# A Fourier layer and two feed-forward blocks: table loads placed behind tiles, weight conversion placed later, planner wait 130 to 210

## The chip, the cores and the metric

The kernel runs on one core of one Trainium2 chip, as one launch. The metric is the device time of that launch in microseconds, lower being better. TensorE is called PE, VectorE DVE, ScalarE ACT, GpSimd POOL and SyncE SP, as in the profile.

## What is computed

Three layers in a row, on `x` of 4 x 3072 x 256 in float32:

```python
X = np.fft.rfft(x, axis=1)
Yr = Xr @ w_r - Xi @ w_i + b_r;  Yi = Xr @ w_i + Xi @ w_r + b_i
Y = soft_threshold(Yr, 0.01) + 1j * soft_threshold(Yi, 0.01)
y = np.fft.irfft(Y, n=3072, axis=1)
h = y @ w_in;  x2 = (h - tanh(h)) @ w_out
xk, xr = token_shift_mix(x2, mu_k), token_shift_mix(x2, mu_r)
out = sigmoid(xr @ w_r2) * (relu(xk @ w_k) ** 2 @ w_v)
```

## The kernel before

The work falls into three parts. The transform runs over four batches (`b`). Both Fourier transforms are products with tables: a transform of 3072 is split into 96 x 32. For each batch:

- `reg_a` (L435), stage A: eight loads of `x` (`load_x`, L391, issued by SP), for each two products with the table `f_sb`, each evacuated by ACT into one half of a tile `at` (L464), which is written to HBM (`adr`, L468; in batch 0 issued by ACT, in the later ones by SP). PE writes to two banks `a` in turn. Batch 0 takes plain float32 products, later batches a split into two parts (`xa`, `xb`).
- `reg_q` (L470): twelve loads of `adr` in another layout, the tiles `q` (L475, SP). Each reads what all eight `adr` writes of its batch have written, so the first one waits for the last write.
- `reg_unit` (L479), twelve units. PE multiplies `q` by the table `t` into a bank `g`; ACT and DVE split it into `xh` and `xl` (two buffers each); PE multiplies these by the weights `wh`, `wl` into a bank `y`; DVE adds `bias` (L529, L532) and applies the threshold; ACT and DVE split that into `zh` and `zl`; PE multiplies by the table `b` into a bank `v`; ACT evacuates it, and SP writes it to `vdr` (L555).
- `reg_ap` (L557): loads of `vdr` in a third layout, products with `e_sb`, writes of `ydr`.

Then follow the two feed-forward blocks (`reg_pair`, `reg_m2`), each over 24 chunks of 512 tokens, with products of 128x128 by 128x256 and 128x512. Meanwhile `reg_conv` (L597) takes the float weights apart, sixteen of them during the transform (raw loads by POOL, L613, DVE work, and writes by SP).

The tables come in seven groups (`groups`): `t2`, `t0`, `t4`, `t6`, `t10`, `t14`, `t18` for the first product of a unit and `b2`, `b0`, ... for its last; the number is the first pair of rows in the group, and units 3 and 4 (counted from 0) use `t6`, 5 and 6 `t10`, 7 and 8 `t14`, 9 to 11 `t18`. All of them, the two weights of the transform (a tile `v` each, split into `wh` and `wl` at L424 and L425), the four bias loads and `e_sb` are loaded by POOL.

The order of the instructions on each engine is made by a planner (`_Plan`, L149). Each operation has an engine, a cost, a priority number and the operations it depends on; the planner places them in a simulated time, in which a result is taken to be usable by another engine `SEM` = 130 ns after its end (L146). Only the order on each engine comes from the plan. What an instruction waits for on the chip is set by the tiles that it reads and writes. The entries that the kernel adds to `deps` by hand for the loads, at the end of the function (`early`, `load_t`, `load_b`), are known to the planner alone:

```python
for n, o in enumerate(early):
    o.deps.add(xt[0, 1 + n][0].readers[0])
for n, (g0, _) in enumerate(groups):
    p = UNITS.index(g0 // 2)
    for o, c in ((load_t[n], 4), (load_b[n], 6)):
        o.deps.add(first_mm[0, p - 2] if p > 1 else xt[0, c][0].readers[0])
```

Of the kernel before, what the change touches and what calls it, by code (L numbers as in the profile page):

```python
# [8 lines left out]
F32 = mybir.dt.float32  # L9
F32R = mybir.dt.float32r  # L10
I32 = mybir.dt.int32
ACTF = mybir.ActivationFunctionType
# [7 lines left out]
NP = 24  # L20
# [125 lines left out]
SEM = 130  # L146
# [165 lines left out]
def fourier_moe_kernel(tc, x, w_r, w_i, b_r, b_i, w_in, w_out, mu_k, mu_r, w_k, w_v, w_rr, c_f, c_e, c_t, c_b, out, nb=B, ydump=None):  # L312
# [22 lines left out]
    def tile_(pool_, shape, dtype, tag, bufs=1, ordered=True):  # L335
        return _Tile(pool_, shape, dtype, tag, bufs, ordered)
# [65 lines left out]
    wst, early = [], []  # L402
    for q, w in enumerate((w_r, w_i)):
        t = tile_(pl, [128, 2, D], F32, "v", 4)
        wst.append(t)
        dma("pool", lambda t=t, w=w: pool.dma_start(out=t(), in_=w.rearrange("(h p) e -> p h e", p=128)), -90, [t], [], 262144)
        early.append(plan.ops[-1])
    for o, r0, r1, src in ((bias, 0, 64, b_r), (bias, 64, 128, b_i), (bias0, 0, 65, b_r), (bias0, 65, 128, b_i)):
        dma("pool", lambda o=o, r0=r0, r1=r1, src=src: pool.dma_start(out=o()[r0:r1], in_=src.partition_broadcast(r1 - r0)), -59.5, [o], [], 65536)
    dma("pool", lambda: pool.dma_start(out=e_sb(), in_=c_e), -59.4, [e_sb], [], 36864)  # L410
    load_t, load_b = [], []

    def reg_tables(n):
        g0, g1 = groups[n]
        dma("pool", lambda: pool.dma_start(out=t_sb[n](), in_=c_t[:, g0:g1]), g0 / 2 - 60 + n, [t_sb[n]], [], 65536 * (g1 - g0))
        load_t.append(plan.ops[-1])
        dma("pool", lambda: pool.dma_start(out=b_sb[n](), in_=c_b[:, g0:g1]), -60 + n * 0.1, [b_sb[n]], [], 131072 * (g1 - g0))
        load_b.append(plan.ops[-1])

    for n in range(len(groups)):  # L420
        reg_tables(n)
    for q in range(2):
        cols = slice(q * D, q * D + D)
        op("act", c_act(512, False), lambda q=q, cols=cols: act.activation(out=wh()[:, :, cols], in_=wst[q](), func=ACTF.Copy), -50, [wh], [wst[q]])  # L424
        op("dve", c_dve(512), lambda q=q, cols=cols: dve.tensor_tensor(out=wl()[:, :, cols], in0=wst[q](), in1=wh()[:, :, cols].bitcast(F32), op=ALU.subtract), -50, [wl], [wst[q], wh])  # L425
# [9 lines left out]
    def reg_a(b):  # L435
        for c in range(8):
            a = tile_(px, [NP * 4, 4, D], F32, "at", AB)
# [39 lines left out]
    first_mm = {}  # L477

    def reg_unit(b, pos):  # L479
# [18 lines left out]
        first_mm[b, pos] = plan.ops[-1]  # L498
# [6 lines left out]
        op("act", c_act(128 * n, False), lambda: act.activation(out=xl()[:, 0:2 * n, 0:64], in_=xl()[:, 0:2 * n, 128:192].bitcast(F32), func=ACTF.Copy, scale=-1.0), z0 - K["x"], [xl], [])  # L505
        if u == 0:
            for o, src in ((xh0, xhc), (xl0, xlc)):
                for c0, k0, sc in ((1, 65, -1.0), (65, 1, 1.0)):
                    op("act", c_act(126, False), lambda o=o, src=src, c0=c0, k0=k0, sc=sc: act.activation(out=o()[:, :, c0:c0 + 63], in_=src[1]()[:, 0:2, k0:k0 + 63].bitcast(F32), func=ACTF.Copy, scale=sc), z0 - K["x"], [o], [src[0]])
# [85 lines left out]
    RAW0, RAW1 = 14, 6  # L595
# [51 lines left out]
    reg_q(0)  # L647
    for b in range(nb):
        for i in range(NU):
            reg_unit(b, i)  # L650
        if b == 0:
            for n, o in enumerate(early):
                o.deps.add(xt[0, 1 + n][0].readers[0])
            for n, (g0, _) in enumerate(groups):
                p = UNITS.index(g0 // 2)
                for o, c in ((load_t[n], 4), (load_b[n], 6)):
                    o.deps.add(first_mm[0, p - 2] if p > 1 else xt[0, c][0].readers[0])
# [394 lines left out]
```

## Time and profile before

| | us |
|---|---|
| median of three runs | 2008.94 (2005.75 to 2009.99) |
| the profiled execution, its own time | 2006.93 |
| its span, first to last instruction | 2005.1 |
| PE busy in the span | 1961.8 (98%) |
| DVE busy | 1599.4 (80%) |
| ACT busy | 1476.9 (74%) |
| POOL busy | 22.9 (1%) |

The profile is one execution. A busy PE is one that has a matmul in flight; the rest of the span, 43.3 us, is time in which PE had nothing to run. The granted clock is the share of TensorE's full 2.4 GHz that it was given, where 0.5 is 1.2 GHz. A wait is put down to what ended last. "us to landing" counts from the issue of a transfer to its completion.

### The profile page before, as it was taken

The page shows a single profiled execution, that of the slowest core. Times are in us where ns is not written, and L with a number is a line of the kernel's source. Part 1 is how long each engine was busy: PE and PEld are TensorE (multiplying, and loading weights), DVE is VectorE, ACT ScalarE, POOL GpSimd, SP SyncE. Part 2 cuts the span into 40 slices and gives each one's busy share as a digit, 9 for nine tenths or more (in the row PEclk, how much of TensorE's full clock was granted, in tenths as well). Part 3 has the DMA queues.
Part 4 walks back from the last instruction along what each step waited for, and adds up shares of the span by engine and source line. Part 5 has one row for each costly group of instructions (what it writes and reads, how often), then busy time and mean ns, then how long its engine had stood idle before and what let it go on. Part 6 is the DMA issues. An engine that isn't in the chain of part 4 may idle for free.

```text
span 2005.1 us, 36620 instructions
## 1 busy us (share of the span) xinstructions
PE 1961.8 (98%) x13760; PEld 1822.3 (91%) x13760; DVE 1599.4 (80%) x3107; ACT 1476.9 (74%) x3166; POOL 22.9 (1%) x42
## 2 busy tenths in 40 slices
PE   5999999999999999999999999999999999999998
PEld 3899989888888888888888888888999999999998
DVE  1688897788887878887878897779988888888885
ACT  3657566777777777777777787778877777777774
POOL 2000000000000000000000000000000000000000
PEclk8999999999999999999999999999999999999999
DMA  9699786511010101010101120001211111111101
GB/s 311 197 288 295 242 264 217 179 48 55 29 47 24 37 22 48 32 38 22 38 22 48 38 69 22 22 11 35 60 44 50 48 47 47 47 47 47 47 22 33
DMA packets 96194, 162.37 MB, mean 81 GB/s; under 512 B 11510, under 2 KB 56675, under 8 KB 96016
## 3 DMA queue, kind: packets, MB, share of 16 engines
q1 hardware_dynamic: 91008, 142.95, 22.8%
q0 software_dynamic: 4112, 13.93, 2.4%
q10 hardware_dynamic: 896, 3.15, 0.4%
q8 instruction: 108, 1.77, 0.4%
q14 instruction: 70, 0.57, 0.1%
HBM read 90.52 MB, written 69.47 MB: 80 GB/s over the span
## 4 chain that ended last, share of the span: by engine, by line
PE 89%; DVE 5%; DMA 3%; ACT 2%; issue 1%; SPq 0%; ACTq 0%; DVEq 0%
PE v L319 39%; PE y L319 20%; PE g L319 17%; PE a L319 14%; DVE hs L840 1%; DVE hs L799 1%; DVE yl L348 1%; DMA x<-in_x_dram 1%; DMA adr<-at 1%; DVE gl L348 1%; DMA ydr<-yt 0%; DMA out_dram<-ob 0%; DVE zl L348 0%; DMA vp<-vdr 0%; DMA yr<-ydr 0%
## 5 line engine op out<-in xcount | busy, mean ns | idle before, releaser
L345 ACT ACTIVATE gh<-hs 128x512 fp32r<-128x512 f32 x504 | 317.2, 629 | 139.2 <-PE v L319 131.4
L348 DVE TENSOR_TENSOR gl<-hs,gh 128x512 fp32r<-128x512 f32 x504 | 345.1, 685 | 79.5 <-ACT gh L345 79.1
L796 ACT ACTIVATE p<-g 128x256 f32<-128x256 f32 x864 | 318.7, 383 | 92.8 <-PE g L319 75.0
L840 DVE TENSOR_TENSOR hs<-hs,th 128x512 f32<-128x512 f32 x384 | 264.4, 689 | 122.1 <-ACT th L839 115.1
L319 PE MATMUL v<-gh,wl 128*128 128x512 f32 x768 | 303.6, 395 | 0.0
L319 PE MATMUL v<-gh,wh 128*128 128x512 f32 x768 | 303.3, 395 | 0.0
L319 PE MATMUL v<-gl,wh 128*128 128x512 f32 x768 | 300.0, 391 | 0.0
L839 ACT ACTIVATE th<-hs 128x512 f32<-128x512 f32 x384 | 241.5, 630 | 76.2 <-DVE hs L799 71.6
L799 DVE TENSOR_TENSOR hs<-y,p 128x256 f32<-128x256 f32 x588 | 241.4, 420 | 37.1 <-PE y L319 25.8
L319 PE MATMUL v<-ah,gh 128*128 128x256 f32 x768 | 217.5, 283 | 0.5 <-DVE ob L1004 0.5
L319 PE MATMUL v<-al,gh 128*128 128x256 f32 x768 | 217.3, 283 | 0.0
L319 PE MATMUL v<-ah,gl 128*128 128x256 f32 x768 | 217.3, 283 | 0.0
L319 PE MATMUL g<-yh,ah 128*128 128x256 f32 x648 | 183.2, 283 | 0.1
L319 PE MATMUL g<-yh,al 128*128 128x256 f32 x648 | 182.8, 282 | 0.0
L319 PE MATMUL g<-yl,ah 128*128 128x256 f32 x648 | 182.5, 282 | 0.0
L319 PEld LDWEIGHTS v<-gl,wh 128*128 128x128 f32 x768 | 144.4, 188 | 33.4
L319 PEld LDWEIGHTS v<-gh,wh 128*128 128x128 f32 x768 | 145.2, 189 | 18.1
L319 PEld LDWEIGHTS v<-gh,wl 128*128 128x128 f32 x768 | 145.2, 189 | 16.0
L319 PE MATMUL y<-yh,ah 128*128 128x256 f32 x496 | 149.8, 302 | 2.6 <-ACT hs L824 1.0
L319 PEld LDWEIGHTS v<-ah,gh 128*128 128x128 f32 x768 | 147.4, 192 | 0.8 <-DVE ob L1004 0.7
L319 PEld LDWEIGHTS v<-al,gh 128*128 128x128 f32 x768 | 147.4, 192 | 0.0
L319 PEld LDWEIGHTS v<-ah,gl 128*128 128x128 f32 x768 | 147.4, 192 | 0.0
(179 smaller groups left out, 4875.9 us busy)
## 6 DMA issues: line engine op xcount, KB each, us to landing
x<-in_x_dram SPq DMA_DIRECT2D x32, 384.0 KB, 5.2
q<-adr SPq DMA_DIRECT2D x48, 256.0 KB, 5.8
vdr<-v SPq DMA_DIRECT2D x48, 256.0 KB, 3.6
vp<-vdr SPq DMA_DIRECT2D x32, 384.0 KB, 6.3
ydr<-yt SPq DMA_DIRECT2D x64, 192.0 KB, 4.5
yr<-ydr SPq DMA_DIRECT2D x24, 512.0 KB, 4.0
xdr<-x SPq DMA_DIRECT2D x24, 512.0 KB, 3.1
xs<-xdr SPq DMA_DIRECT2D x20, 608.0 KB, 4.3
```

The costliest lines, as they stand in the source:

```text
L319: pe.matmul(out=o, lhsT=l, rhs=r, start=st, stop=en, **kw)
L345: op("act", c_act(n, psum), lambda: act.activation(out=o[1](), in_=i[1](), func=ACTF.Copy), prio, [o[0]], [i[0]])
L348: op("dve", c_dve(n), lambda: dve.tensor_tensor(out=o[1](), in0=i[1](), in1=h[1]().bitcast(F32), op=ALU.subtract), prio, [o[0]], [i[0], h[0]])
L796: op("act", c_act(HK, True), lambda: act.activation(out=o(), in_=p()[:, 0:HK], func=ACTF.Copy), prio, [o], [p])
L799: op("dve", c_dve(HK), lambda: dve.tensor_tensor(out=t()[:, half * HK:half * HK + HK], in0=p()[:, 0:HK], in1=s(), op=ALU.add), prio, [t], ...
L839: op("act", c_act(CK, False), lambda th=th, hs=hs: act.activation(out=th(), in_=hs(), func=ACTF.Tanh), z0, [th], [hs])
L840: op("dve", c_dve(CK), lambda th=th, hs=hs: dve.tensor_tensor(out=hs(), in0=hs(), in1=th(), op=ALU.subtract), z0, [hs], [th])
```

## The change

Five things are altered.

1. A helper `pool_after` puts a copy of one element of a given tile into a tile `gate` on POOL (L407 of the changed kernel). The loads that follow it in POOL's order start after that copy. The table, weight, bias and `e_sb` loads are spread behind nine such copies: three read tiles `at` of batch 0, one the first `q`, five the `xh` of units 0, 1, 3, 5 and 7.
2. The entries in `deps` that did this in the plan alone are gone.
3. The two weights are converted with priority -2 in place of -50.
4. `SEM` is 210 in place of 130, for every operation of the kernel.
5. `RAW0`, which says at which unit the plan lets the raw weight loads begin, is 12 in place of 14.

```diff
--- before.py
+++ after.py
@@ -143,7 +143,7 @@
     __slots__ = ("eng", "dur", "lat", "emit", "deps", "prio", "creates", "users", "nleft", "start", "end", "idx", "ready", "frees", "nbytes")
 
 
-SEM = 130
+SEM = 210
 
 
 class _Plan:
@@ -399,30 +399,32 @@
 
     for c in range(8):
         load_x(0, c)
-    wst, early = [], []
-    for q, w in enumerate((w_r, w_i)):
-        t = tile_(pl, [128, 2, D], F32, "v", 4)
-        wst.append(t)
-        dma("pool", lambda t=t, w=w: pool.dma_start(out=t(), in_=w.rearrange("(h p) e -> p h e", p=128)), -90, [t], [], 262144)
-        early.append(plan.ops[-1])
-    for o, r0, r1, src in ((bias, 0, 64, b_r), (bias, 64, 128, b_i), (bias0, 0, 65, b_r), (bias0, 65, 128, b_i)):
-        dma("pool", lambda o=o, r0=r0, r1=r1, src=src: pool.dma_start(out=o()[r0:r1], in_=src.partition_broadcast(r1 - r0)), -59.5, [o], [], 65536)
-    dma("pool", lambda: pool.dma_start(out=e_sb(), in_=c_e), -59.4, [e_sb], [], 36864)
-    load_t, load_b = [], []
-
-    def reg_tables(n):
+    wst = [tile_(pl, [128, 2, D], F32, "v", 4) for _ in range(2)]
+
+    def pool_after(t, view):
+
+        g = tile_(pl, [1, 1], F32, "gate", 2)
+        op("pool", 100, lambda: pool.tensor_copy(out=g(), in_=view(t())), -60, [g], [t])
+        return plan.ops[-1]
+
+    def pool_load(o, emit, nbytes, gate):
+        dma("pool", emit, -60, [o], [], nbytes, after=[gate] if gate else [])
+
+    def load_w(q, gate):
+        w = (w_r, w_i)[q]
+        pool_load(wst[q], lambda: pool.dma_start(out=wst[q](), in_=w.rearrange("(h p) e -> p h e", p=128)), 262144, gate)
+
+    def load_bias(gate):
+        for o, r0, r1, src in ((bias, 0, 64, b_r), (bias, 64, 128, b_i), (bias0, 0, 65, b_r), (bias0, 65, 128, b_i)):
+            pool_load(o, lambda o=o, r0=r0, r1=r1, src=src: pool.dma_start(out=o()[r0:r1], in_=src.partition_broadcast(r1 - r0)), 65536, gate)
+
+    def load_t(n, gate):
         g0, g1 = groups[n]
-        dma("pool", lambda: pool.dma_start(out=t_sb[n](), in_=c_t[:, g0:g1]), g0 / 2 - 60 + n, [t_sb[n]], [], 65536 * (g1 - g0))
-        load_t.append(plan.ops[-1])
-        dma("pool", lambda: pool.dma_start(out=b_sb[n](), in_=c_b[:, g0:g1]), -60 + n * 0.1, [b_sb[n]], [], 131072 * (g1 - g0))
-        load_b.append(plan.ops[-1])
-
-    for n in range(len(groups)):
-        reg_tables(n)
-    for q in range(2):
-        cols = slice(q * D, q * D + D)
-        op("act", c_act(512, False), lambda q=q, cols=cols: act.activation(out=wh()[:, :, cols], in_=wst[q](), func=ACTF.Copy), -50, [wh], [wst[q]])
-        op("dve", c_dve(512), lambda q=q, cols=cols: dve.tensor_tensor(out=wl()[:, :, cols], in0=wst[q](), in1=wh()[:, :, cols].bitcast(F32), op=ALU.subtract), -50, [wl], [wst[q], wh])
+        pool_load(t_sb[n], lambda: pool.dma_start(out=t_sb[n](), in_=c_t[:, g0:g1]), 65536 * (g1 - g0), gate)
+
+    def load_b(n, gate):
+        g0, g1 = groups[n]
+        pool_load(b_sb[n], lambda: pool.dma_start(out=b_sb[n](), in_=c_b[:, g0:g1]), 131072 * (g1 - g0), gate)
 
     fh = tile_(pt, [N1, 128], F32R, "fh")
     fl = tile_(pt, [N1, 128], F32R, "fl")
@@ -434,7 +436,7 @@
 
     def reg_a(b):
         for c in range(8):
-            a = tile_(px, [NP * 4, 4, D], F32, "at", AB)
+            a = at[b, c] = tile_(px, [NP * 4, 4, D], F32, "at", AB)
             for h in range(2):
                 p = bank("a")
                 t, tx = xt[b, c]
@@ -473,8 +475,6 @@
             t = tile_(pt, [128, 2, D], F32, "q", NU)
             qt[b, i] = t
             dma("sp", lambda t=t, u=u: sp.dma_start(out=t(), in_=rows[u]), base(b) + i - K["q"], [t], [adr[b]], 262144)
-
-    first_mm = {}
 
     def reg_unit(b, pos):
         n = 2
@@ -495,7 +495,6 @@
                     mm(px_()[:, o:o + 128], qs()[:, k, dh * 128:dh * 128 + 128], t_sb[g]()[:, ti, :], True, True)
 
         op("pe", 448 * n, e, z0 - K["b"], [px_], [qs] + [t_sb[g] for g, _ in ts_])
-        first_mm[b, pos] = plan.ops[-1]
         x3 = cut(px_, lambda r: r.rearrange("p (k c) -> p k c", k=4)[:, 0:2 * n])
         xhc = cut(xh, lambda r: r[:, 0:2 * n, 64:192])
         xlc = cut(xl, lambda r: r[:, 0:2 * n, 64:192])
@@ -503,6 +502,14 @@
         lo(xlc, x3, xhc, 256 * n, z0 - K["x"])
         op("act", c_act(128 * n, True), lambda: act.activation(out=xh()[:, 0:2 * n, 0:64], in_=x3[1]()[:, :, 64:128], func=ACTF.Copy, scale=-1.0), z0 - K["x"], [xh], [px_], seq=False)
         op("act", c_act(128 * n, False), lambda: act.activation(out=xl()[:, 0:2 * n, 0:64], in_=xl()[:, 0:2 * n, 128:192].bitcast(F32), func=ACTF.Copy, scale=-1.0), z0 - K["x"], [xl], [])
+        if b == 0 and pos in (0, 1, 3, 5, 7):
+            gate = pool_after(xh, lambda r: r[0:1, 0, 64:65].bitcast(F32))
+            n_ = (0, 1, 3, 5, 7).index(pos) + 2
+            if n_ > 2:
+                load_t(n_, gate)
+            load_b(n_, gate)
+            if pos == 3:
+                pool_load(e_sb, lambda: pool.dma_start(out=e_sb(), in_=c_e), 36864, gate)
         if u == 0:
             for o, src in ((xh0, xhc), (xl0, xlc)):
                 for c0, k0, sc in ((1, 65, -1.0), (65, 1, 1.0)):
@@ -592,7 +599,7 @@
     wdr = [_Tile(dram, None, None, None, 1, fixed=wdr_t[i]) for i in range(NW)]
 
     EARLY = 16
-    RAW0, RAW1 = 14, 6
+    RAW0, RAW1 = 12, 6
 
     def reg_conv(i):
         src, split = raws[i]
@@ -645,16 +652,27 @@
     op("pe", 3400, spin, -100, [spare], [warm])
     reg_a(0)
     reg_q(0)
+    corner = lambda r: r[0:1, 0, 0:1]
+    gate = pool_after(at[0, 1], corner)
+    load_t(0, gate)
+    for q in range(2):
+        load_w(q, gate)
+    gate = pool_after(at[0, 4], corner)
+    load_t(1, gate)
+    load_b(0, gate)
+    gate = pool_after(at[0, 7], corner)
+    load_t(2, gate)
+    gate = pool_after(qt[0, 0], corner)
+    load_bias(gate)
+    load_b(1, gate)
+    for q in range(2):
+        cols = slice(q * D, q * D + D)
+        op("act", c_act(512, False), lambda q=q, cols=cols: act.activation(out=wh()[:, :, cols], in_=wst[q](), func=ACTF.Copy), -2, [wh], [wst[q]])
+        op("dve", c_dve(512), lambda q=q, cols=cols: dve.tensor_tensor(out=wl()[:, :, cols], in0=wst[q](), in1=wh()[:, :, cols].bitcast(F32), op=ALU.subtract), -2, [wl], [wst[q], wh])
+
     for b in range(nb):
         for i in range(NU):
             reg_unit(b, i)
-        if b == 0:
-            for n, o in enumerate(early):
-                o.deps.add(xt[0, 1 + n][0].readers[0])
-            for n, (g0, _) in enumerate(groups):
-                p = UNITS.index(g0 // 2)
-                for o, c in ((load_t[n], 4), (load_b[n], 6)):
-                    o.deps.add(first_mm[0, p - 2] if p > 1 else xt[0, c][0].readers[0])
         if b + 1 < nb:
             for c in range(8):
                 load_x(b + 1, c)
```

What it does to the order of the instructions is shown at three places.

POOL at the start of the program; the numbers behind the names tell buffers apart. Before, the weights and tables stand one behind the other:

```order
L406 DMA v_136<-in_w_r_dram 128x2x256
L406 DMA v_147<-in_w_i_dram 128x2x256
L415 DMA t2_163<-in_c_t_dram 128x256
L415 DMA t0_170<-in_c_t_dram 128x256
L417 DMA b2_182<-in_c_b_dram 128x512
L417 DMA b0_188<-in_c_b_dram 128x512
L417 DMA b4_236<-in_c_b_dram 128x512
L417 DMA b6_248<-in_c_b_dram 128x1024
L415 DMA t4_256<-in_c_t_dram 128x256
```
Now the first nine rows behind the memset are

```order
L407 COPY gate_135<-at_128 1x1
L423 DMA t2_139<-in_c_t_dram 128x256
L415 DMA v_145<-in_w_r_dram 128x2x256
L415 DMA v_152<-in_w_i_dram 128x2x256
L407 COPY gate_171<-at_159 1x1
L423 DMA t0_174<-in_c_t_dram 128x256
L427 DMA b2_181<-in_c_b_dram 128x512
L407 COPY gate_202<-at_198 1x1
L423 DMA t4_204<-in_c_t_dram 128x256
```
and the next eleven, from the gate on the first `q`:

```order
L407 COPY gate_220<-q_206 1x1
L419 DMA bias_227<-in_b_r_dram 64x256
L419 DMA bias0_240<-in_b_r_dram 65x256
L427 DMA b0_250<-in_c_b_dram 128x512
L407 COPY gate_263<-xh_238 1x1
L427 DMA b4_266<-in_c_b_dram 128x512
L407 COPY gate_285<-xh_248 1x1
L423 DMA t6_288<-in_c_t_dram 128x512
L419 DMA bias_227<-in_b_i_dram 64x256
L427 DMA b6_316<-in_c_b_dram 128x1024
L419 DMA bias0_240<-in_b_i_dram 63x256
```
The bias loads, which were first, now stand behind the gate on the first `q` and, for their second halves, behind the gate on the second unit's `xh` and the load of `t6`.

PE where the units of batch 0 begin; `g`, `y` and `v` are the three products of a unit. Before:

```order
L319 MATMUL g_222<-t2_163,q_208 128x128 x4
L319 MATMUL g_229<-t0_170,q_210 128x128 x4
L319 MATMUL y_258<-wh_180,xh_238 128x256 x4
L319 MATMUL y_258<-wl_185,xh_238 128x256 x4
L319 MATMUL y_258<-wh_180,xl_242 128x256 x4
...
L319 MATMUL v_327<-zh_321,b2_182 128x256 x2
L319 MATMUL v_327<-zl_323,b2_182 128x256
L319 MATMUL v_327<-zh_321,b2_182 128x256 x2
L319 MATMUL v_327<-zl_323,b2_182 128x256
L319 MATMUL v_347<-zh_341,b0_188 128x256 x2
L319 MATMUL v_347<-zl_343,b0_188 128x256
L319 MATMUL g_351<-t4_256,q_212 128x128 x4
```
Now:

```order
L319 MATMUL g_222<-t2_139,q_206 128x128 x4
L319 MATMUL g_231<-t0_174,q_208 128x128 x4
L319 MATMUL g_258<-t4_204,q_210 128x128 x4
L319 MATMUL y_269<-wh_176,xh_238 128x256 x4
L319 MATMUL y_269<-wl_183,xh_238 128x256 x4
L319 MATMUL y_269<-wh_176,xl_244 128x256 x4
...
L319 MATMUL g_345<-t6_288,q_212 128x128 x4
L319 MATMUL g_356<-t6_288,q_214 128x128 x4
L319 MATMUL y_366<-wh_176,xh_318 128x256 x4
L319 MATMUL y_366<-wl_183,xh_318 128x256 x4
...
L319 MATMUL v_414<-zh_381,b2_181 128x256 x2
```
A third unit's first product stands ahead of the first `y`, and the first `v` has moved from directly behind the second unit's `y` to behind two more `g` and the third unit's `y`.

ACT near the end of stage A of batch 0. Before:

```order
L464 ACTIVATE at_174<-a_167 96x512
L468 DMA adr_61<-at_138 96x1024
L468 DMA adr_61<-at_149 96x1024
L424 ACTIVATE wh_180<-v_136 128x2x256
L468 DMA adr_61<-at_156 96x1024
L468 DMA adr_61<-at_165 96x1024
L464 ACTIVATE at_174<-a_172 96x512
L424 ACTIVATE wh_180<-v_147 128x2x256
L468 DMA adr_61<-at_174 96x1024
```
Now:

```order
L466 ACTIVATE at_167<-a_161 96x512
L470 DMA adr_61<-at_159 96x1024
L670 ACTIVATE wh_176<-v_145 128x2x256
L466 ACTIVATE at_167<-a_169 96x512
L470 DMA adr_61<-at_167 96x1024
L466 ACTIVATE at_188<-a_178 96x512
L670 ACTIVATE wh_176<-v_152 128x2x256
L466 ACTIVATE at_188<-a_186 96x512
```
The first conversion stands behind the eleventh of the sixteen evacuations, as before, the second behind the thirteenth in place of the twelfth. The writes of `adr` that stood behind the eleventh evacuation and the first conversion are now issued ahead of both. On PE, DVE, ACT and SP the orders of the two kernels also differ from here to the end; the number and kind of the instructions on these four engines are the same.

## Rows read from the trace of the kernel before

**Rows 1.** Windows: busy time (instructions) by engine, then granted clock, DMA share, GB/s.
```profile
5.20:24.20 19.00, 15.70 (x32) 5.29 (x32) 1.38 (x2) 10.53 (x18) 7.37 (x14) 1.00 1.13 317
24.20:36.40 12.20, 0.00 (x0) 0.00 (x0) 0.00 (x0) 0.00 (x0) 1.07 (x2) 0.57 1.06 414
...
39.70:60.00 20.30, 16.28 (x101) 15.19 (x102) 8.36 (x15) 8.23 (x20) 0.00 (x0) 0.83 0.76 220
60.00:200.00 140.00, 138.47 (x1074) 132.67 (x1073) 112.99 (x208) 94.10 (x201) 4.31 (x7) 1.00 0.84 265
200.00:400.00 200.00, 193.18 (x1524) 186.54 (x1523) 161.54 (x321) 129.48 (x282) 5.86 (x8) 0.99 0.71 227
400.00:1960.00 1560.00, 1556.75 (x10712) 1441.96 (x10711) 1293.33 (x2521) 1212.61 (x2598) 0.00 (x0) 1.00 0.13 39
1960.00:2005.10 45.10, 37.61 (x310) 37.14 (x309) 21.47 (x43) 19.86 (x43) 0.00 (x0) 0.97 0.13 32
```

**Rows 2.** Chain of work in its first 60 us: start us, us, what.
```profile
24.20 12.17 DMA adr<-at
36.39 3.19 DMA q<-adr
...
39.72 3.62 PE g L319 x16
```

**Rows 3.** DMA, 1.0 to 36.4 us: total; POOL's queue q0; landing of one weight load.
```profile
DMA packets 3684, 11.80 MB, mean 333 GB/s; under 512 B 599, under 2 KB 708, under 8 KB 3684
...
q0 software_dynamic: 1780, 5.46, 47.9%
...
v<-in_w_i_dram POOLq DMA_DIRECT2D x1, 256.0 KB, 11.0
```

**Rows 4.** PE's waits before 60 us: us in total, times, longest.
```profile
PE a L319 <- DMA x<-in_x_dram: 2.6, 5, 0.8
...
PE v L319 <- ACT zh L345: 1.8, 1, 1.8
PE g L319 <- ACT xh L504: 1.2, 1, 1.2
```

**Rows 5.** Timeline of POOL: start us, us, its load issues.
```profile
1.28 1.26 POOL L409 DMA_DIRECT2D bias<-in_b_r_dram  x2 [0.34 <-issue]
...
24.97 0.53 POOL L613 DMA_DIRECT2D raw<-in_moe_w_in_dram  x1
...
117.68 0.62 POOL L613 DMA_DIRECT2D raw<-in_moe_w_in_dram  x1 [92.18 <-DVE cl L617]
```

**Rows 6.** Timeline of ACT in stage A: an evacuation and a weight conversion.
```profile
8.36 0.59 ACT L464 ACTIVATE at<-a 96x512 f32<-96x512 f32 x1 [0.43 <-PE a L319]
...
18.56 0.63 ACT L424 ACTIVATE wh<-v 128x512 fp32r<-128x512 f32 x1 [0.31 <-ACT at L464]
```

**Rows 7.** DMA issues, 60 to 200 us: count, KB each, median us to landing.
```profile
x<-in_x_dram SPq DMA_DIRECT2D x17, 384.0 KB, 4.8
adr<-at SPq DMA_DIRECT2D x16, 384.0 KB, 4.0
q<-adr SPq DMA_DIRECT2D x24, 256.0 KB, 5.5
...
raw<-in_moe_w_in_dram POOLq DMA_DIRECT2D x7, 512.0 KB, 6.3
```

**Rows 8.** Timeline, 68 to 80 us: PE's g products and ACT's first xh behind them.
```profile
68.49 1.95 PE L319 MATMUL g<-t,q 128*128 128x128 f32 x16
...
75.99 1.06 PE L319 MATMUL g<-t,q 128*128 128x128 f32 x8
69.95 0.58 ACT L345 ACTIVATE xh<-g 128x512 fp32r<-128x512 f32 x1
```

**Rows 9.** Page, costliest groups: busy, mean ns of one, idle before.
```profile
L345 ACT ACTIVATE gh<-hs 128x512 fp32r<-128x512 f32 x504 | 317.2, 629 | 139.2 <-PE v L319 131.4
L348 DVE TENSOR_TENSOR gl<-hs,gh 128x512 fp32r<-128x512 f32 x504 | 345.1, 685 | 79.5 <-ACT gh L345 79.1
```

## The prediction

> **What bounds the kernel now.** I read the busy time by stretches first [rows 1]. From 400 us to 1960 us PE is busy 1556.75 of 1560 us, so neither feed-forward block has more than 3.3 us to give. The transform, 60 to 400 us, leaves PE idle for 1.5 and 6.8 us. The end (1960 to 2005.1) holds 7.5 us, behind the last product; the last instructions of all engines are the same kinds in both orders, so it stays. The largest hole is at the start: from 24.2 to 39.7 us no product runs at all.
>
> What fills that hole is in the chain of work [rows 2]: the last write of `adr` is issued at 24.20 us and lands 12.17 us later, the first `q` behind it takes 3.19 us, and PE starts at 39.72 us. An `adr` write issued later in the run lands in 4.0 us [rows 7]. The reader should see why the first batch's takes three times as long: the transfer engines are full (share 1.06, 414 GB/s) while PE is idle [rows 1], and of the 11.80 MB moved by then 5.46 MB are POOL's [rows 3], issued from 1.28 us to 24.97 us without a pause that matters [rows 5]. Before the first `q` PE needs `x` (8 x 0.393 = 3.15 MB), `adr` (as much) and, for the first products, few of POOL's loads. So the start is bound by transfers that nobody needs yet.
>
> **The change, part by part.**
>
> *The gates.* Each copy reads a tile, so unlike the entries in the plan it holds POOL on the chip. Ahead of the gate on the first `q` POOL now issues `t2`, `t0`, `t4` (3 x 0.131 MB), two weights (2 x 0.262) and `b2` (0.262): 1.18 MB. 5.46 - 1.18 = 4.28 MB leave the stretch; at the 414 GB/s of rows 1 that is 10.3 us, so the last `adr` would land at 36.4 - 10.3 = 26.1 us. A second bound is latency: PE's waits for `x` (2.6 us [rows 4]) go, as `x` has the engines nearly alone, so the last evacuation ends at 24.2 - 2.6 = 21.6 us, and with 4.0 us for the write [rows 7] that gives 25.6 us. I take the later one, 26.1, and for `q` 3.3 us more as now: PE starts at 29.4 in place of 39.7 us. **-10.3 us**. Good end: 25.6 with some 0.5 us off the landing of `q`, -11.3. Bad end: see the weights.
>
> *The copies themselves.* The trace shows no such copy; a bound from below is 0, from above one load issue of 0.53 us [rows 5]. Behind them on POOL stand loads alone. Priced where a load is late.
>
> *The weights.* The first gate opens when the third evacuation ends (8.36 + 0.59 = 8.95 us [rows 6]), so the second weight is issued near 11 us. ACT converts in order between evacuations; the first conversion stood at 18.56 us. If the loads land in some 5 us like an `x` later on [rows 7], they are there by 16 us and cost nothing: the cover is the rest of stage A. If they took the 11.0 us of now [rows 3], the second would land at 22 us and hold ACT, then PE behind its two banks, for about 3 us. Taken: 0, because the queue that made those 11.0 us is gone; bad end +3.3.
>
> *The first units.* From 39.7 to 60 us PE is idle for 20.3 - 16.28 = 4.0 us [rows 1], of which 1.8 us is a `v` waiting for `zh` and 1.2 us a `g` waiting for `xh` [rows 4]. In the new order a third `g` precedes the first `y`, and the first `v` stands behind two `g` and a `y` more: a `y` pair of products is work enough to cover either wait. **-2.5 us**, between 0 and -4.0. New here: the second halves of the bias are issued behind the gate on the second `xh` and `t6`, and DVE's first add waits for them with all of DVE behind it. The add should be some us late; it is the same `g` and `y` work on PE that covers it. 0, bad end +2.0.
>
> *The later tables.* The tight one is `t14`: its gate is the `xh` of unit 5, and PE wants it for unit 7. Now that `xh` ends at 69.95 + 0.58 = 70.53 us and the product of unit 7 starts at 75.99 us [rows 8]: 5.5 us apart, with the same PE work between them in the new order. Less copy and issue (0.62 us beside a busy DVE [rows 5]) some 4.7 us remain. Landing of 256 KB: 384 KB take 4.8, a queued 256 KB `q` 5.5, POOL's 512 KB 6.3 us [rows 7]. I take 5.2: **+0.5 us**, ends 0 and +2.0. The Trainium skill's page "DMA: Bandwidth & Descriptors" (section "Anatomy of one DMA — SWDGE (gpsimd) path") fits a POOL load as 2.0 us plus its bytes at 436 GB/s. By that the estimate for `t14` is 2.6 us, the 0.5 us would go and the sum be 0.5 us lower; rows 7, with other traffic about, are all longer. `t18` is wanted about three times as far behind its gate, and the `b` tables behind two further products, so these cost 0. The raw loads come last on POOL, but the second one is held until 117.68 us by DVE's work on the first [rows 5], so the first may come tens of us later: 0.
>
> *The clock.* After the hole PE ran at the lower level, 1.2 GHz, for a while: 16 `g` products took 3.62 us [rows 2] and later 1.95 us [rows 8]; a granted mean of 0.83 over 20.3 us [rows 1] is 3.4 us lost. The idle stretch shrinks from 15.5 to some 8 us. I take 0 (the clock falls again), good end -3.4.
>
> *`SEM` and `RAW0`.* They move instructions everywhere but add none. What the planner leaves out of its costs can be read: it costs a 512-wide DVE operation at 602 ns and the ACT one at 519 ns; they take 685 and 629 ns [rows 9]. So 83 to 110 ns of an assumed 130 are used before the hand-over, and 210 stands nearer the truth: consumers move further behind producers. That should remove a little of the 8.3 us of idle in the transform and can hardly help where 3.3 us are left. Taken 0; ends -4 and +4 for the transform, -1 and +3 for the rest.
>
> **Sum.** -10.3 - 2.5 + 0.5 = -12.3 us against the profiled execution's 2006.93: 1994.6. The median of the runs, 2008.94, lies 2.0 us above that execution, so for a median I add these: **1996.6 us**.
>
> **Rivals.**
>
> *Collision, +7.9 us: 2004.5.* What left the start must still be moved. Behind the first `q` POOL issues 1.57 MB (bias, `b0`, `b4`, `t6`, `b6`) while eleven `q` and six `x` are queued. If these shared the engines so that the units wait for all of it, 1.57 MB at 317 to 414 GB/s [rows 1] are 5.0 to 3.8 us, 4.4 in the middle, and with the bad ends of the bias (2.0) and of `t14` (1.5 more) 7.9 us. For: the share was 0.76 and 0.84 after 39.7 us [rows 1]. Against: a sixth to a quarter of the engines' time is spare there, and a unit needs one `q`, not twelve.
>
> *The feed-forward blocks lose, slower: 2020.6.* The plan is new for all 48 chunk passes between 400 and 1960 us, 32.5 us each. If the greater assumed wait interleaves two chains so that PE waits 0.5 us in each pass, that is 24 us. It decides from 12.3 / 48 = 0.26 us a pass. For: DVE is busy 83% and ACT 78% there [rows 1], with little room to recover. Against: PE waits 3.3 us in all of it now, and a longer assumed wait puts more work between producer and consumer.
>
> *The gates hold nothing: 2008.9.* If a copy did not hold the loads behind it, as the plan's entries do not now, only the order would change. Against: the copy reads what ACT writes.
>
> *POOL is starved by DVE: 1999.* Issues on POOL took 0.53 us beside an idle DVE and 0.62 us beside a busy one [rows 5]. If each issue waited out a DVE operation of 0.69 us [rows 9], `t14` would come 1.4 us later (copy and issue) and the bias 1 us beyond its cover: +2.4 us. The Trainium skill's page "SBUF — State Buffer" warns of this: GpSimd shares a port pair with DVE, held whole by whoever has it, so that loads issued by GpSimd wait for their descriptors. The rows show a tenth of a us of it.
>
> **How the numbers follow.** Chances: the forecast 0.72, collision 0.13, slower blocks 0.07, idle gates 0.04, starved POOL 0.04. About 0.2% (4.0 us) is what this measurement can tell from no change, so faster means below 2004.9. The forecast, the starved POOL and half of the collision lie there: 0.83. Same holds the rest of the collision and the idle gates: 0.10. Slower 0.07. Range: the good ends (-1.0, -1.5, -0.5, -3.4, -4, -1) sum to -11.4 and the bad (+3.3, +2.5, +2.0, +1.5, +4, +3) to +16.3; they won't meet, so two thirds of the one and half of the other: 1989 to 2005, which takes in the collision and leaves out the slower blocks and the idle gates.
>
> **What would show it.** Right: the last `adr` lands near 26 us, some 4 to 5 us after its issue; PE's first `g` near 29.4 us; no wait of PE for `x`; PE's idle time from 400 to 1960 us within 3 us of now. Each step wrong: ACT waits for a weight before 22 us; PE waits for a `t` near 65 us or DVE for a bias near 38 us; 39.7 to 60 us still has 4 us of idle, moved. The prediction fails if PE starts after 34 us, or if PE's idle time behind 400 us grows by more than 8 us.

## The result and the profile after

The changed kernel takes **1975.65 us** (median of 4, 1974.37 to 1975.88) against 2009.47 beside it (2005.75 to 2011.58): a ratio of 0.9832 [0.9817, 0.9847], 33.8 us less. The forecast was 1996.6, the low end of its range 1989. The sign was right, the size was not: the gain is over twice the forecast. One execution of e8 below, at 3170.25 us, was in a slow state and is left out of its figures.

Windows of the changed kernel, by the same stages as [rows 1] (columns as there):

```profile
5.20:21.50 16.30, 15.23 (x32) 4.96 (x32) 1.38 (x2) 9.71 (x17) 3.57 (x8) 1.00 1.04 322
21.50:29.40 7.90, 0.01 (x1) 0.04 (x1) 0.00 (x0) 0.59 (x1) 0.64 (x3) 0.70 0.68 249
29.40:60.00 30.60, 28.06 (x181) 26.75 (x182) 14.92 (x26) 13.90 (x32) 6.70 (x15) 0.80 1.08 276
60.00:200.00 140.00, 135.12 (x1030) 129.33 (x1029) 111.40 (x208) 89.06 (x192) 8.13 (x15) 0.98 0.89 285
200.00:400.00 200.00, 195.14 (x1540) 188.31 (x1540) 163.13 (x320) 135.38 (x296) 5.14 (x7) 1.00 0.70 218
400.00:1930.00 1530.00, 1528.92 (x10666) 1430.41 (x10665) 1283.62 (x2509) 1190.85 (x2582) 0.00 (x0) 1.00 0.13 40
1930.00:1973.80 43.80, 37.02 (x304) 36.41 (x303) 22.44 (x44) 20.56 (x45) 0.00 (x0) 0.96 0.10 25
```

The hole between stage A and the first `g` is 7.9 us in place of 15.5. In the feed-forward blocks PE is busy for all but 1.1 us of 1530, before for all but 3.3 of 1560 [rows 1]: the busy time shows hardly a gain there. Yet the gain is there, as the times of the writes tell. Timeline of the queue SP, the second and the twenty-first write of `xdr`, before and then after:

```profile
464.12 0.56 SPq L864 DMA_DIRECT2D xdr<-x  x1
...
1282.02 0.55 SPq L864 DMA_DIRECT2D xdr<-x  x1
```

```profile
454.01 0.55 SPq L882 DMA_DIRECT2D xdr<-x  x1
...
1257.94 0.56 SPq L882 DMA_DIRECT2D xdr<-x  x1
```

Nineteen chunks of block 1 take 817.90 us before and 803.93 after: 43.05 and 42.31 us each. In block 2 the second and the twentieth chunk's output writes, before and then after:

```profile
1460.83 4.97 SPq L1011 DMA_DIRECT2D out_dram<-ob  x8
...
1908.31 93.71 SPq L1011 DMA_DIRECT2D out_dram<-ob  x40
```

```profile
1435.98 5.23 SPq L1029 DMA_DIRECT2D out_dram<-ob  x8
...
1876.76 94.28 SPq L1029 DMA_DIRECT2D out_dram<-ob  x40
```

Eighteen chunks take 447.48 and 440.78 us: 24.86 and 24.49 each. (After the change these writes come in threes, 26.9, 23.4 and 23.1 us apart, so only a multiple of three intervals gives their mean; the expectations below go by 17 intervals, which give 24.87 and 24.35.) That is 14.0 + 6.7 = 20.7 us in the chunks counted. From the first `xdr` write to the end of the program it is 1583.6 us before and 1562.1 after: **21.5 us in the blocks**. The first `xdr` write comes 9.75 us earlier (421.47 to 411.72): that is what the transform gives. Together these are the 31.3 us by which the spans of the profiled executions differ.

The start, to be held against [rows 2] and [rows 3]: timeline of the changed kernel, and its DMA from 1.0 to 26.5 us (all packets, POOL's queue, a weight load).

```profile
22.13 0.31 ACTq L470 DMA_DIRECT2D adr<-at  x1
26.51 0.92 SPq L477 DMA_DIRECT2D q<-adr  x2
29.39 3.75 PE L319 MATMUL g<-t,q 128*128 128x128 f32 x16 [7.93 <-DMA q<-adr]
```

```profile
DMA packets 2352, 7.52 MB, mean 295 GB/s; under 512 B 368, under 2 KB 464, under 8 KB 2352
...
q0 software_dynamic: 448, 1.18, 15.5%
...
v<-in_w_i_dram POOLq DMA_DIRECT2D x1, 256.0 KB, 7.4
```

POOL moved the 1.18 MB that the prediction counted, the `q` loads go out at 26.51 us (26.1 forecast) and PE starts at 29.39 (29.4 forecast). The last `adr` is issued at 22.13 us and takes 4.4 us to land, with the transfer engines busy for a share of 0.74: of the prediction's two bounds it was the second, latency, that set the time, and the two lay within 0.5 us of each other. PE's waits before 60 us, as in [rows 4]:

```profile
PE g L319 <- DMA q<-adr: 7.9, 1, 7.9
PE a L319 <- ACT at L466: 1.0, 1, 1.0
...
PE g L319 <- ACT xh L503: 1.0, 1, 1.0
PE v L319 <- ACT zh L345: 0.9, 1, 0.9
PE a L319 <- DMA x<-in_x_dram: 0.6, 1, 0.6
PE v L319 <- DVE zl L348: 0.6, 1, 0.6
```

### The profile page after: what moved, and what is told of

Its sections match the earlier page's. It is cut to its first block, busy times and chain, and to the rows that moved or that the text cites. A ratio compares the mean times of both kernels' runs of the same rounds, so it can differ in the third digit from the quotient of the medians.

```text
span 1973.8 us, 36575 instructions
## 1 busy us (share of the span) xinstructions
PE 1943.1 (98%) x13760; PEld 1819.6 (92%) x13760; DVE 1597.2 (81%) x3107; ACT 1462.1 (74%) x3166; POOL 24.6 (1%) x51
## 3 DMA queue, kind: packets, MB, share of 16 engines
q1 hardware_dynamic: 91008, 142.95, 23.4%
## 4 chain that ended last, share of the span: by engine, by line
PE 87%; DVE 2%; DMA 2%; ACT 0%; issue 0%; DVEq 0%; SPq 0%; ACTq 0%
PE v L319 41%; PE y L319 17%; PE g L319 16%; PE a L319 13%; DMA out_dram<-ob 0%; DMA raw<-in_moe_w_in_dram 0%; DVE hs L817 0%; DMA vp<-vdr 0%; DMA adr<-at 0%; DVE x L941 0%; DVE hs L986 0%; DVE gl L348 0%; DVE yt L704 0%; DMA q<-adr 0%; DVE zl L348 0%
## 5 line engine op out<-in xcount | busy, mean ns | idle before, releaser
L319 PEld LDWEIGHTS v<-gl,wh 128*128 128x128 f32 x768 | 144.4, 188 | 33.4
L319 PE MATMUL y<-yh,ah 128*128 128x256 f32 x496 | 140.9, 284 | 1.6 <-ACT hs L842 1.3
```

Source lines behind the costliest of these rows:

```text
L319: pe.matmul(out=o, lhsT=l, rhs=r, start=st, stop=en, **kw)
```

## Where the blocks' time was hidden

A `y` or `a` product consists of three matmuls; the first one's weight load waits until DVE's add `hs` has read the bank. PEld and PE by line, 470 to 1250 us, before and then after (busy, mean ns of one, idle before and its releaser):

```profile
L319 PEld LDWEIGHTS y<-yh,ah 128*128 128x128 f32 x292 | 55.0, 188 | 13.0 <-DVE hs L799 7.7 <-DVE xs L910 0.2
L319 PEld LDWEIGHTS a<-yh,ah 128*128 128x128 f32 x288 | 54.1, 188 | 12.8 <-DVE hs L799 8.0
...
L319 PE MATMUL y<-yh,ah 128*128 128x256 f32 x292 | 87.8, 301 | 0.9 <-DVE hs L799 0.2
```

```profile
L319 PEld LDWEIGHTS y<-yh,ah 128*128 128x128 f32 x295 | 56.1, 190 | 3.9
L319 PEld LDWEIGHTS a<-yh,ah 128*128 128x128 f32 x294 | 55.9, 190 | 6.2
...
L319 PE MATMUL y<-yh,ah 128*128 128x256 f32 x295 | 83.0, 281 | 0.0
```

The wait stands with PEld, 15.7 us in 62 waits of 0.2 us or more, and hardly with PE. A timeline of a place with a shorter delay in the kernel before shows how PE loses time without looking idle (weight loads, DVE's add, then PE):

```profile
699.80 0.19 PEld L319 LDWEIGHTS g<-yl,ah 128*128 128x128 f32 x1
700.00 0.19 PEld L319 LDWEIGHTS y<-yh,ah 128*128 128x128 f32 x1
...
699.52 0.42 DVE L799 TENSOR_TENSOR hs<-y,p 128x256 f32<-128x256 f32 x1
...
699.92 0.28 PE L319 MATMUL g<-yl,ah 128*128 128x256 f32 x1
700.04 0.35 PE L319 MATMUL y<-yh,ah 128*128 128x256 f32 x1
700.22 0.28 PE L319 MATMUL y<-yh,al 128*128 128x256 f32 x1
```

Loads follow one another every 0.12 us; this one comes 0.20 us after the last, once DVE is done (699.52 + 0.42). The matmul behind it is then recorded with 0.35 us in place of 0.28, and the next starts 0.18 us later in place of 0.12. Since records of 0.28 us overlap at a spacing of 0.12, PE does not look idle. Nor does PEld here: its last load ended at 699.99. So PEld's idle time points to the place but is not the loss. That can be counted from the starts of the matmuls. From 470 to 1250 us the second matmul of a `y` or `a` product starts 0.16 us or more behind the first in 164 of 580 products before, and in none of 589 after; what these lie above 0.12 us adds up to 11.6 us. The periods differ by 13.4 us over this stretch.

In block 2 PEld hardly waits. Its waits before, 400 to 1260 us and, below them, 1440 to 1840 us (after the change, both lists are empty):

```profile
PEld y L319 <- DVE hs L799: 8.4, 34, 0.4
PEld a L319 <- DVE hs L799: 8.0, 31, 1.4
```

```profile
PEld v L319 <- DVE ob L1004: 0.7, 1, 0.7
PEld y L319 <- DVE hs L799: 0.4, 1, 0.4
PEld y L319 <- ACT hs L824: 0.2, 1, 0.2
```

What is left there is a longer record of the first matmul of a `y` (293 to 297 ns on average from 1440 to 1840 us, 282 to 283 for the other two; after, 283 to 285). That points to late loads there too, but what each of them waits for was not followed: in block 2 it is shown that the assumed wait makes the loss (e1 and e6 below), not through which tile.

The Trainium skill's page "Perfetto Trace Analysis" (section "Identifying the Most-Contended Engine") says that matmul busy time is not a good measure of how close TensorE is to its limit, and names the weight loads' busy share as one of two better ones. The trace agrees for both blocks together: PEld was busy 92.4% (1441.96 of 1560) in [rows 1] and 93.5% (1430.41 of 1530) after. In block 2 alone it does not: from 1440 to 1840 us PEld was busy 397.03 of 400 us before and 399.92 after, and the chunks became 1.5% shorter.

## The experiments

Medians in us; ratio to the kernel before on the same chip; first `g` and first `xdr` write of the profiled execution; chunk periods as above, in block 2 over eighteen chunks. For the kernel before: 39.7, 421.5, 43.05, 24.86. The changed kernel, e1 to e4, e5 to e8, e9 to e12 and e13 to e15 are five sessions, in which the kernel before took 2007.58 to 2010.13 us, so medians of two sessions compare to some 2.5 us.

| run | us | ratio [95%] | first g | xdr | block 1 | block 2 |
|---|---|---|---|---|---|---|
| changed | 1975.65 | 0.9832 [0.9817, 0.9847] | 29.4 | 411.7 | 42.31 | 24.49 |
| e1 | 1985.11 | 0.9889 [0.9875, 0.9904] | 39.5 | 422.8 | 42.30 | 24.48 |
| e2 | 2007.06 | 0.9996 [0.9986, 1.0006] | 30.6 | 424.7 | 43.03 | 24.87 |
| e3 | 1992.38 | 0.9925 [0.9908, 0.9941] | 39.4 | 423.6 | 42.46 | 24.67 |
| e4 | 1991.21 | 0.9930 [0.9902, 0.9958] | 38.9 | 420.0 | 42.51 | 24.65 |
| e5 | 1993.13 | 0.9905 [0.9886, 0.9924] | 34.0 | 424.6 | 42.30 | 24.48 |
| e6 | 1999.91 | 0.9948 [0.9930, 0.9967] | 33.4 | 417.8 | 43.08 | 24.89 |
| e7 | 1991.17 | 0.9908 [0.9889, 0.9927] | 29.6 | 424.5 | 42.31 | 24.48 |
| e8 | 2001.33 | 0.9949 [0.9930, 0.9968] | 34.0 | 418.8 | 43.04 | 24.82 |
| e9 | 1980.84 | 0.9855 [0.9840, 0.9871] | 40.9 | 416.7 | 42.29 | 24.49 |
| e10 | 1986.33 | 0.9880 [0.9854, 0.9905] | 31.6 | 416.2 | 42.41 | 24.55 |
| e11 | 1976.50 | 0.9831 [0.9809, 0.9852] | 31.5 | 414.5 | 42.33 | 24.44 |
| e12 | 1974.10 | 0.9820 [0.9804, 0.9836] | 29.3 | 411.6 | 42.30 | 24.51 |
| e13 | 1972.66 | 0.9823 [0.9808, 0.9838] | 32.3 | 409.3 | 42.30 | 24.48 |
| e14 | 1972.85 | 0.9819 [0.9804, 0.9833] | 32.5 | 410.1 | 42.30 | 24.49 |
| e15 | 1983.00 | 0.9876 [0.9852, 0.9900] | 32.4 | 427.6 | 42.30 | 24.48 |

The periods repeat to 0.1 us. The transform does not: e6, e10 and e11 run the transform in the order of the changed kernel, and their first `g` comes at 33.4, 31.6 and 31.5 us. A single `xdr` time is good to some 6 us; medians say more.

**e1, the assumed wait alone.** Kernel before with `-SEM = 130` `+SEM = 210`.

> The kernel before with the planner's assumed wait SEM at 210 instead of 130, and nothing else. Theory 1 (the longer assumed wait moves matmuls away from the VectorE add that frees their PSUM bank, so that weight loads stop waiting some tens of ns in both feed-forward blocks; worth 31.3 - 9.2 = 22 us there, the early loads the other 10): PE's first g still at 39.7 us, the first xdr write at 421 (+-2), the period of a chunk in block 1 at 42.3 us instead of 43.0, of block 2 at 24.35 instead of 24.87, the time 1986 (1983 to 1990). Theory 2 (the blocks gain because the new start shifts the plan or because RAW0 is 12; SEM does little): periods stay at 43.0 and 24.87, the time 2005 to 2012. Theory 3 (any other order of the blocks moves them by as much, either way): periods change by another amount than 0.7 and 0.5 us.

Theory 1 holds: the periods are those of the changed kernel and 22.5 us go. No second matmul comes late in block 1 any more.

**e2, everything but the assumed wait.** Changed kernel with `-SEM = 210` `+SEM = 130`.

> The changed kernel with SEM back at 130; the copies that gate the loads, the later conversion of the weights and RAW0 = 12 stay. Theory 1: first g at 29.4 us, first xdr write at 411 to 413, periods 43.0 and 24.87, PE's weight loads of the first y and a products wait again for VectorE's hs add; the time 1998 to 2000. Theory 2: periods 42.3 and 24.35, the time 1975 to 1979. Theory 3: periods neither.

Half a miss. The blocks are back at 43.03 and 24.87 as theory 1 has it, and PEld waits for `hs` again (15.4 us from 470 to 1250 us; 161 of 581 second matmuls late). But the early start (30.6) is gone by the first `xdr` write: 2007.06, no gain. The parts don't add.

**e3 and e4, whose wait.** Kernel before; in the planner, by engine, `+LAT = {'dve': 210}` (e3) or `+LAT = {'pe': 210, 'act': 210}` (e4), `-o.lat = lat` `+o.lat = LAT.get(eng, SEM)`.

> The kernel before with the assumed wait at 210 for what VectorE releases alone, 130 for the other engines. Theory 1: what matters is PE behind VectorE's add into hs; periods 42.3 and 24.35, time 1985 to 1990, like the run with 210 everywhere. If the longer wait behind PE or ScalarE matters instead: periods 43.0 and 24.87, time 2005 to 2010.

> The kernel before with the assumed wait at 210 for what TensorE and ScalarE release, 130 for VectorE, GpSimd and SyncE. Theory 1: weight loads keep waiting for VectorE's hs add, periods 42.9 to 43.0 and 24.8 to 24.9, time 2004 to 2009. If the longer wait behind PE or ScalarE matters: 42.3 and 24.35, time 1986.

e4 is a miss, and e3 falls short of its theory 1: either half brings most of the gain, neither all of it. So it is not DVE's own hand-over alone that was too short; the runs fit the round trip, PE to DVE and back to PE, that was planned at 2 x 130 ns. e4 raises ACT's wait together with PE's, so PE's share alone is not shown. PEld of e4 by line, 470 to 1250 us, with 2.1 us where 8.0 were:

```profile
L320 PEld LDWEIGHTS a<-yh,ah 128*128 128x128 f32 x293 | 55.4, 189 | 7.2 <-DVE hs L800 2.1
...
L320 PE MATMUL y<-yh,ah 128*128 128x256 f32 x295 | 84.4, 286 | 0.0
```

**e10 and e11, the dose.** Changed kernel with its own constant from the first operation of the blocks on: `+SEM_FF = 170` (e10) or `+SEM_FF = 300` (e11), `-lat=SEM` `+lat=None`, `+plan.lat = SEM_FF`.

> The changed kernel with the assumed wait at 170 in both feed-forward blocks, 210 in the transform. Theory 1 in its sharper form (what counts is the assumed round trip from TensorE over VectorE's or ScalarE's operation and back, twice the assumed wait: 260 before, 420 after, 340 in the two runs with a part at 210): periods like those runs, 42.4 to 42.5 and 24.4 to 24.6, the time 1979 to 1983. If any order other than that of 130 does: periods 42.3 and 24.35 or something else, no order by size.

> The changed kernel with the assumed wait at 300 in both feed-forward blocks, 210 in the transform. Theory 1: with 210 hardly a weight load waits any more, so there is nothing left to gain: periods 42.2 to 42.4 and 24.3 to 24.4, the time 1974 to 1978. If the planner then runs out of work to put between (a bank held longer): periods above 42.5 and 24.5, the time over 1981. If the gain goes on with the size: periods under 42.1 and 24.2, the time under 1972.

By round trip the periods are 43.05 / 24.86 at 260 ns, 42.41 / 24.55 at 340 (e3 and e4, at the same sum, 0.05 to 0.12 more), 42.31 / 24.49 at 420 and 42.33 / 24.44 at 600. The late second matmuls of block 1, counted as above, are 164, 35 (e3 51, e4 56), 0 and 8. So the gain comes by size and ends where hardly a load comes late any more. e10's time is above what was expected; the chunks counted explain 3.0 of the 10.7 us above the changed kernel (19 x 0.10 + 18 x 0.06). The first `xdr` write of its profiled execution is 4.5 us later, and its four executions lie between 1981.87 and 1990.47.

**e5 and e6, the two places apart.** The same constants: 130 in the transform and 210 in the blocks (e5), and the reverse (e6).

> The changed kernel with the assumed wait at 130 for all operations of the transform (and the early weight conversions) and 210 for those of both feed-forward blocks. Theory 1 (the two places gain separately: in the blocks 22 us from the assumed wait alone, in the transform 10 us only when the early loads are held back and the assumed wait is long): the transform as in the run of the changed kernel with 130, first xdr write 422 to 425; periods 42.3 and 24.35; the time 1984 to 1987. Theory 2 (the gain of the early start is lost wherever one plan ends badly, by chance): the first xdr write anywhere from 411 to 425, the time 1975 to 1987.

> The changed kernel with the assumed wait at 210 in the transform and 130 in both feed-forward blocks. Theory 1: first xdr write 410 to 413, periods 43.0 and 24.87, the time 1997 to 2000. If the blocks gain through the state in which the transform leaves them: periods 42.3 and 24.35, the time 1975 to 1978.

The blocks follow their own constant only: 42.30 / 24.48 in e5, 43.08 / 24.89 in e6. e6's time is as expected, though its first `xdr` write is 5 us late; e5's write is as expected, though its median is 6 us above (its profiled execution took 1986.60).

**e7, e8 and e15, RAW0.** Changed kernel with `-RAW0, RAW1 = 12, 6` and `+RAW0, RAW1 = 14, 6` (e7), the same with `SEM = 130` (e8), or `+RAW0, RAW1 = 10, 6` (e15).

> The changed kernel with RAW0 back at 14 (the raw weights are loaded two q loads later) and nothing else. If RAW0 is a by-matter: first g 29.4, first xdr write 411 to 413, the time 1974 to 1978. If RAW0 = 12 carries part of the gain in the transform: first xdr write 414 to 422, the time 1978 to 1986.

> The copies that hold the loads and the later conversion of the weights alone: the changed kernel with SEM at 130 and RAW0 at 14. Theory 1 (with an assumed wait of 130 the transform gives the early start back, whatever RAW0 is): first g 29.4 to 31, first xdr write 420 to 426, the time 2003 to 2009. If RAW0 = 12 was what spoiled the run with 130: first xdr write 411 to 414, the time 1995 to 2000.

> The changed kernel with RAW0 at 10 (the raw weights are loaded two q loads earlier). Theory (RAW0 decides by chance where VectorE's conversion work meets the borders of the batches, and TensorE's pauses there, with the clock that falls behind some of them, decide where the transform ends): first xdr write anywhere between 411 and 425 us, moved by idle time and low clock that the stretches from 180 to 425 us show; the blocks' periods unchanged at 42.3 and 24.35; the time 1974 to 1989. If an earlier load is better in itself: first xdr write under 411.

RAW0 is no by-matter: 14 costs 15.5 us against the changed kernel and 10 costs 7 to 9 (by medians and by ratios), with the blocks unchanged. e15's `xdr` write, 427.6, lies behind the 425 expected, in a profiled execution 7.6 us above its median. e8 falls between its two expectations: with `SEM` at 130, RAW0 = 14 keeps a gain of some 9 us, RAW0 = 12 none (e2). Two places can be read. In e15 the first raw load goes out at 39.52 us (72.49 in the changed kernel), and its conversion stands in DVE's queue among the first units. From 28 to 62 us PE runs 155 matmuls there and stands idle for 10.1 us; in the changed kernel it is 197 and 3.9. Timeline of DVE in e15:

```profile
47.56 0.69 DVE L536 TENSOR_TENSOR t<-y,bias 128x512 f32<-128x512 f32 x1 [3.54 <-DMA bias<-in_b_i_dram]
...
56.12 0.43 DVE L624 TENSOR_SCALAR cq<-raw 128x512 int32<-128x512 int32 x1 [2.67 <-DMA raw<-in_moe_w_in_dram]
```

In e7 PE pauses at the end of the transform and the clock falls behind the pauses. Windows of e7, and below them of the changed kernel:

```profile
340.00:360.00 20.00, 14.28 (x97) 12.21 (x96) 18.36 (x40) 16.35 (x38) 0.00 (x0) 1.00 0.55 166
360.00:376.00 16.00, 15.86 (x74) 15.86 (x75) 6.91 (x14) 6.07 (x12) 0.00 (x0) 0.50 0.76 202
```

```profile
340.00:360.00 20.00, 16.92 (x121) 15.08 (x119) 18.44 (x40) 18.56 (x43) 0.00 (x0) 1.00 0.64 179
360.00:376.00 16.00, 16.00 (x131) 15.49 (x129) 11.24 (x20) 11.58 (x26) 0.00 (x0) 1.00 0.80 250
```

With 5.7 us idle in place of 3.1, 16 us run at 1.2 GHz: 74 matmuls in place of 131, 7 to 8 us lost. That is about half of what e7 lacks. Why RAW0 = 14 makes those pauses longer was not settled.

**e9, copies that hold nothing.** `-in_=view(t())` `+in_=warm()[0:1, 0:1]`; PE, DVE and ACT run the same order.

> The changed kernel, but each of GpSimd's small copies reads a tile that is ready from the start, so that it no longer holds the loads behind it; the order on every engine is the same. Theory 1 (the copies take 10.3 us out of the start because they keep 4.3 MB out of the stretch before the first q): PE's first g back at 38 to 41 us, the last adr landing near 36, the blocks' periods 42.3 and 24.35 as in the changed kernel, the time 1983 to 1990. Rival (the order of the loads and the later conversion of the weights make the early start, not the waiting): first g 29 to 31, the time 1975 to 1978.

The first `g` goes back to 40.9 us, with a wait for `q` of 16.0 us: the holding makes the early start, 11.5 us of it. At the end it is worth 5.2 us by the medians, half of what was expected, and 4.6 by the ratios, whose intervals overlap a little. In e9's own session every execution of e11 and e12, which keep the holding, lies below all of e9's, so the sign is safe and the size is not.

**e12, no low clock.** Behind `reg_q(0)`, in its core: `+spare2 = bank("a")` and, after the last evacuation of stage A, `+mm(spare2()[:, 0:128], warm(), warm(), True, True)` 28 times.

> The changed kernel with 28 idle products of the warm-up kind behind stage A, so that TensorE stays busy from 22 to 28 us, where it now waits for the first q with the granted clock falling to 0.50. Theory (the low clock after the hole costs 9.3 us at half speed, 4.6 us): first g still at 29.4 to 30 us, granted clock 1.00 from there, the 16 early g and first y products in half the time, first xdr write at 405 to 409, the time 1969 to 1973. Rival (the early units wait for transfers anyway, or the gain is given back at the batch borders): first xdr write 410 to 414, the time 1974 to 1978.

Windows of e12: the hole, the first products, a pause, and what follows.

```profile
21.50:29.20 7.70, 6.78 (x57) 6.33 (x56) 0.00 (x0) 0.80 (x2) 0.71 (x2) 1.00 0.78 284
29.20:39.10 9.90, 8.85 (x72) 8.57 (x72) 2.08 (x3) 4.54 (x13) 4.86 (x11) 1.00 0.95 273
39.10:42.70 3.60, 0.06 (x1) 0.00 (x0) 0.00 (x0) 0.00 (x0) 0.00 (x0) 0.87 1.15 348
42.70:48.00 5.30, 5.24 (x24) 5.27 (x25) 4.08 (x8) 1.80 (x4) 1.79 (x4) 0.50 1.09 245
```

The first products run at the full clock, and then PE stops for 3.6 us: the fourth `g` starts at 42.77 us, against 43.03 in the changed kernel, where work at half speed hid the wait. The profile names no releaser for it, but the table fits: `t6` is issued at 32.52 us and takes 10.2 us, so it lands at 42.72 (in the changed kernel 34.38 + 8.6 = 42.98). The rival was right: first `xdr` write at 411.6.

**e13 and e14, t6 and the bias earlier.** `-if n_ > 2:` `+if n_ > 3:`, and `load_t(3, gate)` and `load_bias(gate)` behind `load_t(2, gate)`; e14 adds e12's products, 32 of them.

> The changed kernel with the table t6 and the bias (0.26 MB each) issued behind the third copy, ahead of the first q, in place of behind the copies on the first q and the second xh. Theory (the early start is worth 11.5 us at the first g but 5.2 us at the end because the fourth g then waits for t6, landing near 42.7 us, and VectorE for the bias until 43.1 us): first g 1.3 us later (30.7), no wait of VectorE for the bias, no wait of TensorE at the fourth g, PE idle and low clock between 40 and 62 us gone, first xdr write 408 to 411, the time 1971 to 1974. Rival (the early units are bound otherwise, or the gain is given back at the batch borders): first xdr write 411 to 414, the time 1975 to 1979.

> The same with 32 idle products behind stage A, so that the clock does not fall while TensorE waits for the first q. Theory: now that t6 and the bias are there, the full clock is worth its 3 to 4.6 us: first xdr write 404 to 408, the time 1967 to 1971. Rival: as the run with t6 and the bias early alone.

PE's waits in e13, 28 to 62 us, are down to the first `q` and one `xh`, and DVE's wait for the bias is gone. But the planner also orders the early units anew here, with the fourth `g` at 39.33 us, behind 12 of the 48 `y` matmuls that precede it in the changed kernel, so the run does not tell the loads from the order. PE's waits:

```profile
PE g L319 <- DMA q<-adr: 10.0, 1, 10.0
PE g L319 <- ACT xh L503: 1.0, 1, 1.0
```

The first `g` comes at 32.3 us, later than expected, and the first `xdr` write at 409.3 all the same. 1972.66 is the lowest median here, 3 us below the changed kernel; the intervals of the two ratios overlap, so it is not shown to be faster. e14 adds nothing to it, but it does not test the clock: its products end 2.7 us before the first `q`, and from 32.5 to 40 us the granted clock is 0.77, as in e13 from 32.2 to 40.

## Why the prediction was wrong, by its own steps

- *"So neither feed-forward block has more than 3.3 us to give"*: **this step failed**, and with it "Taken 0" for `SEM`. PE's busy share was read as a bound. The blocks gave 21.5 us (e1 alone 22.5), from weight loads that come late while PE's records overlap; PEld's waits show them in block 1, idle time of neither in block 2. The prediction saw that 130 ns were mostly used up by costs set too low [rows 9], and then put the remedy at nothing because PE looked full. Its own sign for this step, PE's idle time behind 400 us within 3 us of before, came true (1.1 against 3.3 us): it could not show the failure.
- *The gates, -10.3*: right at the first `g` in bytes and in the landing of the last `adr`, though by its second bound. That the start agrees to 0.01 us is luck: the same order started between 29.3 and 33.4 us in e6, e10, e11 and e12. At the end it was not right; there the holding is worth some 5 us (e9).
- *The first units, -2.5*: came in part. From the first `g` to 60 us PE is idle for 2.5 us in place of 4.0, with smaller waits for `xh` and `zh` (1.0 and 0.9, before 1.2 and 1.8) and a new one for `zl` (0.6). "0, bad end +2.0" for the bias: DVE waited 2.3 and 1.0 us for it in the changed kernel and 5.9 in e12, and what that cost in the end was not measured apart. `t6`, for which no term stood there, held the fourth `g`. POOL's loads issued in those units took 6.6 to 12.2 us to land in e12, not the 5.2 us taken for `t14`; they share the transfer engines with twelve `q` and six `x`. This is the collision rival, in the first units and smaller.
- *`t14` +0.5, weights 0*: PE did not wait for any later table; ACT waited 0.3 us for a weight, PE 1.0 for an evacuation. Small, as said.
- *`RAW0`, 0*: failed; 14 in place of 12 is 15.5 us in the changed kernel. With `SEM` at 130 it has the other sign (e8 against e2).
- *The clock, 0*: right for the start, where e12 shows the low clock to be covered. For the rest of the transform no term stood there, and e7 lost 7 to 8 us to it.
- The rival "blocks lose" had the right place and the wrong sign. "Starved POOL" did not show: from 29 to 60 us issues took 0.53 to 0.58 us and a copy 0.17, one of them 0.28.

The sum by runs: 22.5 us from the assumed wait (e1), some 5 from the holding (e9), and some 6 left of 33.8 for RAW0, the loads' order and the later conversion together, which no run takes apart. These do not add in general: with the wait at 130 the same edits give nothing (e2) or, with RAW0 at 14, some 9 us (e8). What sets the transform's end among such plans stays open beyond the two places shown.

## What to carry to other kernels

Where matmul records overlap, ask for the weight loads' waits, for the starts of the matmuls and for the time from one chunk to the next before calling TensorE full; a delay shorter than the overlap does not show as idle time. When the chunks' times come in a pattern, count whole patterns. In a planner, an assumed hand-over that is too short was paid in 164 of 580 products here, and one that is somewhat long cost next to nothing. A gain at the start of a stage is worth only what the stage's next late transfer and its pauses let through: follow it to the stage's last write.

## What was not expected of the hardware

In e12 the granted clock stood at 0.50 for the 5.3 us of work behind a pause of 3.6 us, while the wait of 1 us for `xh` in the stretch ahead of it left it at 1.00. In e7 it stayed at 0.50 for 16 us with PE busy 15.86 of them. A small GpSimd copy that reads a tile holds the loads behind it (e9) and took 0.17 us, one of nine 0.28.
